# Experts 2 to 7: gathered rows transposed by VectorE after a trip through DRAM; second MLP: first two tiles transposed on TensorE

## The chip, the cores and the metric

The kernel runs on one core of one Trainium2 chip. The metric is the device time of one execution in microseconds (us). A profile of one execution stands beside the times; "span" is the time from the first to the last recorded instruction in it. Engines are called TensorE (PE; PEld is its weight load), VectorE (DVE), ScalarE (ACT), GpSimd (POOL) and SyncE (SP, which here only issues DMAs).

## What is computed

Three layers follow each other, all in float32. A linear attention (softmax of q over the head dimension, of k over the sequence) gives x, 2304 rows of 512. A mixture of eight experts with two chosen per row takes x, and a second MLP with a softmax gate and a normalisation takes its result:

```python
# attention: B, H, S, D = 4, 8, 576, 64
kv = np.einsum('bhsd,bhse->bhde', k_s, v)
x = np.einsum('bhsd,bhde->bhse', q_s, kv)          # -> 2304 x 512

# experts: D, F, E = 512, 1024, 8; two experts chosen per row
for e in range(E):
    for k in range(2):
        mask = top2[:, k] == e
        h = np.maximum(x[mask] @ w1[e], 0.0)
        out[mask] += top2_w[mask, k, None] * (h @ w2[e])

# second MLP: 512 -> 1024 -> 512
h = x @ w_in
solu = h * softmax(h)
ln = (solu - mean(solu)) / np.sqrt(var(solu) + 1e-06) * g_ln
out = ln @ w_out
```

## The kernel before

**Splitting.** Every large product is done as three products of float32r parts: an operand is cast to float32r by ScalarE (the high part, names ending in h) and the rest is formed by VectorE (the low part, names ending in l). A product takes high x high, high x low and low x high. TensorE wants both operands with the contracted index on the partitions, so activations must be transposed between layers.

**Expert stage.** Each expert has room for 640 rows, five tiles of 128. `gather_x` fetches a tile's rows from the DRAM tensor xd by an indirect DMA on GpSimd's queue. `xt_tile` transposes it: `transpose_split` does four 128x128 transposes on TensorE into one of two PSUM banks (tile name t), ScalarE casts them to xh, VectorE subtracts to xl (lines 732, 734, 735). The loop `for e in range(1, E)` first runs the first product of expert e in eight parts (`mm1`, line 756: 24 matmuls of 320 columns each), whose results ScalarE and VectorE turn into hh and hl (lines 760, 761), and then the second product in five tiles (`mm2`, line 792: 24 matmuls of 512 columns). Ahead of each of these five tiles stands `xt_tile(e + 1, a)`, the transposition of a row tile for the next expert. Weights come in 512 KB pieces on SyncE's queue (`load_w1`, `load_w2`, lines 146, 152) into four shared raw buffers, and are split by `split_w1` and `split_w2` (lines 161, 162, 167, 168). A background generator, `decode_all`, takes a step at most places of the loop: it loads a piece of the second MLP's weights (tile f, line 193), decodes it on VectorE (lines 201 to 216) and stores it to DRAM (line 217).

**Second MLP.** It runs over 18 tiles of 128 rows in a software pipeline, `for i in range(NC + 3)`. `h_in(i)` is the first product (line 840, 48 matmuls of two halves), `solu(i)` the softmax gate (maximum at line 849, exponential 852, product 855, mean taken off 858), `rstd(i - 1)` the statistics (lines 868 to 878), `x2_trans(i + 1)` the transposition of a later input tile on TensorE, `o_out(i - 3)` the output product (line 923). The gated activations of tile t (name ed, at the end dT) must be transposed before `o_out(t)`. For tiles 0 to 15 that goes through DRAM: `d_write` stores them (line 885), `d_read` reads them back in four DMAs, so that each group of 32 partitions holds its share of the columns (line 890), and `d_back` transposes 32x32 blocks on VectorE (line 896), casts (899) and subtracts (900). For the last two tiles `d_trans` does eight transposes on TensorE instead (line 910).

Every engine works through its own instructions in the order in which the program wrote them, and a DMA queue likewise: an issue that waits holds back what stands behind it. At the end of the expert stage stands a branch for rows that do not fit into 640 places (`overflow`).

Of the kernel before, what the change touches and what calls it, by code (L numbers as in the profile page):

```python
# [8 lines left out]
F32 = mybir.dt.float32  # L9
# [11 lines left out]
NT, DM, FF, E = 2304, 512, 1024, 8  # L21
R = 4
NC = NT // 128
NL = S - 128 * R
KD, KF = DM // 128, FF // 128
NA = 5
# [21 lines left out]
def col_rows(t):  # L48

    j, c = divmod(t, 9)  # L50
    if c == 8:
        return [(64 * u, 64, (2 * j + u) * S + 128 * R, 1) for u in range(2)]
    return [(0, 128, (2 * j + c // R) * S + c % R, R)]

ORDER = """
F:100011101100000000100000000000101111 lk:0 lq:0 lkl:0 lk:1 kr:0 kmt:0 qm:0 lvl:0 km:0:0 klt:0 kl:0 km:0:1 kb:0
# [26 lines left out]
def attn_moe_kernel(ctx: ExitStack, tc: tile.TileContext, q, k, v, w_gate, w_noise, noise,  # L83
                    w1, w2, w_in, w_out, g_ln, out, order=None, stop=False):
    nc = tc.nc
    V, A, P, T, SP = nc.vector, nc.scalar, nc.gpsimd, nc.tensor, nc.sync
# [5 lines left out]
    dram = ctx.enter_context(tc.tile_pool(name="dram", bufs=1, space=DRAM))  # L92
    sb = ctx.enter_context(tc.tile_pool(name="sb", bufs=1))

    def slot(tag, shape, dt, name):
        return sb.tile(shape, dt, tag=tag, name=name)

    def ring(*tags):
        state = [-1]

        def take(shape, dt, name):
            state[0] = (state[0] + 1) % len(tags)
            return slot(tags[state[0]], shape, dt, name)
        return take

    new_raw = ring("R2", "R3", "R0", "R1")
    new_row = ring("S0", "S2", "S4", "S1", "S3")
    new_out = ring("S9", "S8", "S10")
    new_s2 = ring("S5", "S6", "S7", "S11")
    psA = ctx.enter_context(tc.tile_pool(name="psA", bufs=2, space=PSUM))  # L110
    psB = ctx.enter_context(tc.tile_pool(name="psB", bufs=2, space=PSUM))
# [4 lines left out]
    tab = dram.tile([OVT * 128, 2], I32, name="tab")  # L116
    win32 = dram.tile([DM, FF], F32, name="win32")
    wout32 = dram.tile([FF, DM], F32, name="wout32")
    dd = [dram.tile([128, FF], F32, name=f"dd{t}") for t in range(NC - 2)]

    def bank_t():
        return psT.tile([128, 512], F32, tag="t", name="t")
# [4 lines left out]
    def bank_b():  # L127
        return psB.tile([128, 512], F32, tag="b", name="b")
# [13 lines left out]

    def load_w1(e, j):
        t = new_raw([128, KD, 256], F32, "raw")
        src = win32 if e == E else w1[e]
        SP.dma_start(out=t, in_=src[:, 256 * j:256 * j + 256].rearrange("(k p) f -> p k f", p=128))
        raw[1, e, j] = t

    def load_w2(e, j):
# [313 lines left out]
    eTs, xs = {}, {}  # L463
# [68 lines left out]
    Gt = {}  # L532
# [186 lines left out]
    xg = {}  # L719

    def gather_x(e, a):
        t = new_row([128, DM], F32, "xg")
        c = E * a + e
        first = e == 0 and a < TA
        P.indirect_dma_start(out=t, out_offset=None, in_=xd[0:NRA, :] if first else xd, in_offset=bass.IndirectOffsetOnAxis(  # L725
            ap=idxA[:, a:a + 1] if first else idx[:, c:c + 1], axis=0))
        xg[e, a] = t

    def transpose_split(t, hi, lo):
        ps = bank_t()  # L730
        for kk in range(KD):
            T.transpose(ps[:, 128 * kk:128 * kk + 128], t[:, 128 * kk:128 * kk + 128], ident)  # L732
        pv = ps.rearrange("p (k t) -> p k t", k=KD)
        A.copy(hi, pv)  # L734
        V.tensor_sub(lo, pv, hi)  # L735

    XT = {}

    def xt_tile(e, a):
        if a == 0:  # L740
            XT[e] = (slot("XH", [128, KD, CAP], F32R, "xh"), slot("XL", [128, KD, CAP], F32R, "xl"))
        hi, lo = XT[e]
        transpose_split(xg.pop((e, a)), hi[:, :, 128 * a:128 * a + 128], lo[:, :, 128 * a:128 * a + 128])

    hT = {}

# [56 lines left out]
    def col_of(t):  # L803

        return t if t < NC - 2 else 2 * NC - 3 - t
# [39 lines left out]
    def solu(t):  # L845
        pa = hb.pop(t)
        c = col[:, t]
        pf = pa.rearrange("p n f -> p (n f)")
        V.reduce_max(c[:, 0:1], pf, axis=AX, negate=True)  # L849
        ed = new_ed([128, 2, FF], F32, "ed")  # L850
        e, d = ed[:, 0], ed[:, 1]
        A.activation(out=e, in_=pf, func=AF.Exp, bias=c[:, 0:1], accum_out=c[:, 1:2])  # L852
        V.tensor_scalar(c[:, 2:3], c[:, 1:2], 1e-9, None, op0=OP.add)
        V.reciprocal(c[:, 2:3], c[:, 2:3])  # L854
        V.scalar_tensor_tensor(d, pf, c[:, 2:3], e, op0=OP.mult, op1=OP.mult, accum_out=c[:, 3:4])  # L855
        V.tensor_scalar(c[:, 4:5], c[:, 3:4], -1.0 / FF, None, op0=OP.mult)
        if t < NC - 2:
            V.tensor_scalar(d, d, c[:, 4:5], None, op0=OP.add)
        else:
            V.tensor_scalar(e.rearrange("p (k g c) -> p g k c", g=4, k=KF), d.rearrange(  # L860
                "p (g k c) -> p g k c", g=4, k=KF), c[:, 4:5], None, op0=OP.add)
            e, d = d, e
        rsd[t] = e, d, c[:, 7:8]
# [20 lines left out]
    def d_write(t):  # L884
        SP.dma_start(out=dd[t], in_=rsd[t][1])
# [17 lines left out]
    def d_trans(t):  # L903
        d = rsd[t][1]
        dt = new_dT([128, 2, KF, 128], F32R, "dT")
        for i in range(2):
            ps = bank_t()
            for k in range(4):
                c = 512 * i + 128 * k
                T.transpose(ps[:, 128 * k:128 * k + 128], d[:, c:c + 128], ident)  # L910
            pv = ps.rearrange("p (k t) -> p k t", k=4)
            hi, lo = (dt[:, j, 4 * i:4 * i + 4, :] for j in range(2))
            A.copy(hi, pv)
            V.tensor_sub(lo, pv, hi)
        dT[t] = (dt[:, 0], dt[:, 1])

    def o_out(t):
        hi, lo = dT.pop(t)
        pb = bank_b()
        for kk in range(KF):  # L920
            wh, wl = (w[:, kk % 2, :] for w in WO[kk // 2])
            for s, (x, w) in enumerate(((hi, wh), (hi, wl), (lo, wh))):
                T.matmul(pb, lhsT=x[:, kk, :], rhs=w, start=(kk == 0 and s == 0),  # L923
                         stop=(kk == KF - 1 and s == 2))
        y = rsd.pop(t)[2]
        o = new_out([128, DM], F32, "o")
        if t < NC - 1:
            A.activation(out=o, in_=pb, func=AF.Copy, scale=y)
        else:
            A.activation(out=o[:, 0:256], in_=pb[:, 0:256], func=AF.Copy, scale=y)  # L930
            V.tensor_scalar(o[:, 256:512], pb[:, 256:512], y, None, op0=OP.mult)  # L931
        for p0, n, row, st in col_rows(col_of(t)):
            dst = out[row:row + n, :] if st == 1 else out[row - row % S:row - row % S + st * n, :].rearrange(
                "(p r) d -> p r d", r=st)[:, row % S, :]
            SP.dma_start(out=dst, in_=o[p0:p0 + n, :])
# [191 lines left out]
    for e in range(1, E):  # L1127
        for m in range(KF):
            mm1(e, m)
            if m < 4:  # L1130
                split_w2(e, m)
                load_w1(e + 1, m)
            if e + 1 < E and m < NA:
                gather_x(e + 1, m)
            if m >= 3:
                next(bg, None)
            if e == 2 and m == 5:
                pair_gates()
                count_overflow()
        if stop:  # L1140
            return
        for a in range(NA):
            if e + 1 < E:
                xt_tile(e + 1, a)
            mm2(e, a)
            if e < E - 1:
                next(bg, None)
                if a < 4:
                    split_w1(e + 1, a)
                    load_w2(e + 1, a)  # L1150
                continue
            gather_y(a)
            if a < 2:
                for j in (2 * a, 2 * a + 1):
                    split_w1(E, j)
                    load_w2(E, j)
            elif a == 2:
                next(bg, None)
                combine(0)
                split_w2(E, 0)  # L1160
            elif a == 3:
                x2_trans(0)
                combine(1)
                split_w2(E, 1)
# [7 lines left out]
    for i in range(NC + 3):  # L1172
        if i < NC:
            h_in(i)
        if 0 <= i - 1 < NC - 2:
            d_read(i - 1)
        if 0 <= i - 2 < NC - 2:
            d_back(i - 2)
        if 2 <= i < NC - 1:
            x2_trans(i + 1)  # L1180
        if i < NC:
            solu(i)
        if i < NC - 2:
            d_write(i)
        if i == 0:
            x2_trans(2)
        if i < NC - 3:
            combine(i + 3)
        if i == 1:
            split_w2(E, 3)  # L1190
        if 1 <= i <= NC:
            rstd(i - 1)
        if i >= 3:
            o_out(i - 3)
        if i in (NC - 1, NC):
            d_trans(i - 1)
        if i + 5 < NC:
            gather_y(i + 5)
# [31 lines left out]
```

## Time and profile before

| | us |
|---|---|
| three runs, median (lowest to highest) | 815.04 (814.2 to 815.2) |
| the profiled execution | 813.08 |
| span of the profiled execution | 811.3 |
| TensorE busy | 756.5 |
| VectorE busy | 504.0 |
| ScalarE busy | 293.9 |
| GpSimd busy | 147.1 |

The DMA engines move 150 GB/s on average. Times of instructions below are counted from the start of the span. Matmuls overlap: one that is listed with 0.40 us may be followed by the next after 0.23, so that the length of a stretch on TensorE is read from starts, not from durations.

### The profile page before, as it was taken

How to read it: one execution, taken by the hardware profiler on the slowest of the kernel's cores; microseconds unless marked ns; L12 is line 12 of the kernel's file. 1: busy time of each engine (PE TensorE's matmuls, PEld its weight loads, DVE VectorE, ACT ScalarE, POOL GpSimd, SP SyncE). 2: the span in 40 equal slices, each digit the busy share in tenths (PEclk: the TensorE clock that was granted, in tenths of full speed). 3: DMA queues.
4: the chain of work that ended last, by engine and by line, in shares of the span. 5: the costliest groups of instructions: out<-in, count | busy, mean ns of one | idle time of the engine just before them, and what ended most of it. 6: DMA issues, size and time to landing. Idle time of an engine off the chain costs nothing. (4 is left out here: it accounts for less than half of the span.)

```text
span 811.3 us, 12471 instructions
## 1 busy us (share of the span) xinstructions
PE 756.5 (93%) x4918; PEld 682.5 (84%) x4918; DVE 504.0 (62%) x884; ACT 293.9 (36%) x484; POOL 147.1 (18%) x130
## 2 busy tenths in 40 slices
PE   2877859999999999999999999999988999999997
PEld 1776858989889889899899899898777999899986
DVE  5899783335656656657646656555466777767661
ACT  1566531333223223223232332231444444444441
POOL 3584563020110110200100200000341211200000
PEclk9998899999999999999999999999997999999999
DMA  9973444264454443554544452532754645543311
GB/s 266 269 249 118 143 158 143 79 195 156 134 178 130 144 157 129 170 168 128 177 137 141 170 168 79 162 119 90 219 167 156 179 151 164 156 144 130 107 50 39
DMA packets 82974, 122.07 MB, mean 150 GB/s; under 512 B 15072, under 2 KB 53984, under 8 KB 82912
## 3 DMA queue, kind: packets, MB, share of 16 engines
q1 hardware_dynamic: 76832, 101.32, 39.3%
q0 software_dynamic: 6080, 19.93, 8.7%
q8 instruction: 39, 0.64, 0.3%
q14 instruction: 23, 0.19, 0.1%
HBM read 88.72 MB, written 32.51 MB: 149 GB/s over the span
## 5 line engine op out<-in xcount | busy, mean ns | idle before, releaser
L756 PE MATMUL a<-xh,w1h 128*128 128x320 f32 x448 | 138.6, 309 | 1.2 <-DVE hl L761 1.2
L756 PE MATMUL a<-xl,w1h 128*128 128x320 f32 x448 | 138.4, 309 | 0.0
L756 PE MATMUL a<-xh,w1l 128*128 128x320 f32 x448 | 138.4, 309 | 0.0
L792 PE MATMUL b<-w2h,hh 128*128 128x512 f32 x320 | 128.8, 402 | 0.0
L792 PE MATMUL b<-w2h,hl 128*128 128x512 f32 x320 | 126.7, 396 | 0.0
L792 PE MATMUL b<-w2l,hh 128*128 128x512 f32 x320 | 126.3, 395 | 0.0
L760 ACT ACTIVATE hh<-a 128x640 fp32r<-128x640 f32 x56 | 39.5, 706 | 159.9 <-PE a L756 159.9
L725 POOL DMA_INDIRECT xg<-xd,idx x38 | 40.7, 1070 | 304.1 <-PE t L732 294.7
L761 DVE SCALAR_TENSOR_TENSOR hl<-a,hh 128x640 fp32r<-128x640 f32 x56 | 46.1, 823 | 64.8 <-ACT hh L760 64.8
L756 PEld LDWEIGHTS a<-xh,w1h 128*128 128x128 f32 x448 | 84.1, 188 | 1.8 <-DVE hl L761 1.4
L756 PEld LDWEIGHTS a<-xl,w1h 128*128 128x128 f32 x448 | 84.1, 188 | 0.4
L756 PEld LDWEIGHTS a<-xh,w1l 128*128 128x128 f32 x448 | 84.2, 188 | 0.0
L815 POOL DMA_INDIRECT yg<-yd,posi x36 | 37.7, 1048 | 212.4 <-DVE w1l L162 100.1
L792 PEld LDWEIGHTS b<-w2h,hl 128*128 128x128 f32 x320 | 60.0, 187 | 13.9
L792 PEld LDWEIGHTS b<-w2l,hh 128*128 128x128 f32 x320 | 60.2, 188 | 13.0
L792 PEld LDWEIGHTS b<-w2h,hh 128*128 128x128 f32 x320 | 60.2, 188 | 12.6
L840 PE MATMUL a<-w1h,x2h 128*128 128x256 f32 x288 | 58.3, 284 | 7.8 <-ACT x2h L734 7.3
L162 DVE TENSOR_TENSOR w1l<-raw,w1h 128x1024 fp32r<-128x1024 f32 x32 | 38.9, 1222 | 33.5 <-ACT w1h L161 33.5
L840 PE MATMUL a<-w1h,x2l 128*128 128x256 f32 x288 | 57.8, 282 | 0.2 <-DVE x2l L735 0.2
L840 PE MATMUL a<-w1l,x2h 128*128 128x256 f32 x288 | 57.7, 282 | 0.0
L794 DVE COPY yo<-b 128x512 f32<-128x512 f32 x24 | 16.6, 691 | 64.2 <-PE b L792 64.2
L923 PE MATMUL b<-w2x,dT 128*128 128x512 f32 x216 | 54.4, 400 | 0.0
(209 smaller groups left out, 1395.1 us busy)
## 6 DMA issues: line engine op xcount, KB each, us to landing
raw<-in_moe_w_dram SPq DMA_DIRECT2D x64, 512.0 KB
yd<-yo SPq DMA_DIRECT2D x40, 256.0 KB
dd<-ed SPq DMA_DIRECT2D x16, 512.0 KB
dq<-dd SPq DMA_DIRECT2D x64, 128.0 KB
k<-in_k_dram SPq DMA_DIRECT2D x4, 1024.0 KB
q<-in_q_dram SPq DMA_DIRECT2D x4, 1024.0 KB
v<-in_v_dram SPq DMA_DIRECT2D x4, 1024.0 KB
xd<-xr SPq DMA_DIRECT2D x8, 512.0 KB
```

The source lines that it names most:

```text
L162: (pick_engine(20 + j, P, V) if e == 0 else V).tensor_sub(W1l[j], t, W1h[j])
L725: P.indirect_dma_start(out=t, out_offset=None, in_=xd[0:NRA, :] if first else xd, in_offset=bass.IndirectOffsetOnAxis(ap=idxA[:, a:a + 1] ...
L756: T.matmul(pa[:, n, 0:HC], lhsT=a, rhs=b, start=(kk == 0 and s == 0), stop=(kk == KD - 1 and s == 2))
L760: A.activation(out=h2, in_=pa[:, :, 0:HC], func=AF.Relu)
L761: V.scalar_tensor_tensor(l2, pa[:, :, 0:HC], 0.0, h2, op0=OP.max, op1=OP.subtract)
L792: T.matmul(pb, lhsT=x, rhs=y, start=(kk == 0 and s == 0), stop=(kk == KF - 1 and s == 2))
L794: (A.copy if a % 2 else V.tensor_copy)(t, pb)
L815: P.indirect_dma_start(out=r, out_offset=None, in_=yd[0:n, :], in_offset=bass.IndirectOffsetOnAxis(ap=posi[:, c, j:j + 1], axis=0))
L840: T.matmul(pa[:, n, 256 * c:256 * c + 256], lhsT=x[:, kk, :], rhs=w[2 * n + c][:, kk, :], start=(kk == 0 and s == 0 and c == 0), stop=(kk ...
L923: T.matmul(pb, lhsT=x[:, kk, :], rhs=w, start=(kk == 0 and s == 0), stop=(kk == KF - 1 and s == 2))
```

## The change

Two constants come in: EQ = 2 and NP = 2.

For experts EQ to 7, `gather_x` puts the rows into one of three new buffers, which have the names of attention tiles that are no longer in use. `write_x` stores them to DRAM, `read_x` reads them back with four DMAs of 64 KB, one for each group of 32 partitions, and `xt_tile` has VectorE transpose 32x32 blocks into one of two buffers; ScalarE and VectorE then split from there. Since the contracted index lies differently on the partitions in that form, the first weights of these experts are loaded in four DMAs too. In the loop of expert e the write of tile a is issued at part a + 1 of the first product, the read at part a + 3. For tiles 0 to NP - 1 of the second MLP the activations are transposed by `d_trans`, and `o_out` of these two tiles is called one step earlier; in step 4 there is none.

```diff
-        src = win32 if e == E else w1[e]
-        SP.dma_start(out=t, in_=src[:, 256 * j:256 * j + 256].rearrange("(k p) f -> p k f", p=128))
+        src = (win32 if e == E else w1[e])[:, 256 * j:256 * j + 256]
+        if e < EQ or e == E:
+            SP.dma_start(out=t, in_=src.rearrange("(k p) f -> p k f", p=128))
+        else:
+            for g in range(4):
+                SP.dma_start(out=t[32 * g:32 * g + 32], in_=src[128 * g:128 * g + 128].rearrange("(k c) f -> c k f", c=32))
...
-        t = new_row([128, DM], F32, "xg")
+        t = (new_row if e < EQ else new_hop)([128, DM], F32, "xg")
...
+    def write_x(e, a):
+        SP.dma_start(out=xs_d[e, a], in_=xg[e, a])
+
+    def read_x(e, a):
+
+        t = xg[e, a] = new_row([128, DM], F32, "xg")
+        for g in range(4):
+            SP.dma_start(out=t[32 * g:32 * g + 32].rearrange("i (b f) -> i b f", b=4),
+                         in_=xs_d[e, a].rearrange("(b i) f -> i b f", i=32)[:, :, 128 * g:128 * g + 128])
...
-        transpose_split(xg.pop((e, a)), hi[:, :, 128 * a:128 * a + 128], lo[:, :, 128 * a:128 * a + 128])
+        hi, lo = (x[:, :, 128 * a:128 * a + 128] for x in XT[e])
+        t = xg.pop((e, a))
+        if e < EQ:
+            transpose_split(t, hi, lo)
+            return
+        x = slot(("S12", "Gt")[a % 2], [128, KD, 4, 32], F32, "xt")
+        V.transpose(x.rearrange("p k b i -> p b k i"), t.rearrange("p (b k c) -> p b k c", b=4, k=KD))
+        x = x.rearrange("p k b i -> p k (b i)")
+        A.copy(hi, x)
+        V.tensor_sub(lo, x, hi)
...
+            if EQ <= e + 1 < E:
+                if 1 <= m < NA + 1:
+                    write_x(e + 1, m - 1)
+                if 3 <= m:
+                    read_x(e + 1, m - 3)
...
-        if 0 <= i - 1 < NC - 2:
+        if i == 1:
+            d_trans(0)
+        if NP <= i - 1 < NC - 2:
             d_read(i - 1)
-        if 0 <= i - 2 < NC - 2:
+        if NP <= i - 2 < NC - 2:
             d_back(i - 2)
...
-        if i >= 3:
+        if 2 <= i < 2 + NP:
+            o_out(i - 2)
+        if i >= 3 + NP:
             o_out(i - 3)
-        if i in (NC - 1, NC):
+        if i in (NP, NC - 1, NC):
             d_trans(i - 1)
```

How the instructions stand now is shown at three places. Line numbers of the changed kernel are higher by up to 37.

SyncE's queue, loop of expert 1, before: gl are the normalisation's factors, raw a piece of weights, f the first pieces to be decoded, win the decoded ones.

```order
L1092 DMA gl<-in_moe_g_ln_dram 32x8x1 x4
L146 DMA raw<-in_moe_w_dram 128x4x256 x4
L193 DMA f_1932<-in_moe_w_in_dram 128x1024
L193 DMA f_1934<-in_moe_w_in_dram 128x1024
L217 DMA win_78<-dec_1965 128x512
L193 DMA f_2060<-in_moe_w_in_dram 128x1024
```

The same place after; xs are the row tiles of expert 2 in DRAM.

```order
L156 DMA raw<-in_moe_w_dram 32x4x256 x8
L740 DMA xs_0_80<-xg 128x512
L156 DMA raw<-in_moe_w_dram 32x4x256 x4
L740 DMA xs_1_81<-xg 128x512
L156 DMA raw<-in_moe_w_dram 32x4x256 x4
L740 DMA xs_2_82<-xg 128x512
L746 DMA xg<-xs_0_80 32x4x128 x4
L203 DMA f_1980<-in_moe_w_in_dram 128x1024
L203 DMA f_1982<-in_moe_w_in_dram 128x1024
L740 DMA xs_3_83<-xg 128x512
L746 DMA xg<-xs_1_81 32x4x128 x4
```

Between the second and the third piece of weights stands a write, between the fourth and the first f a write and four reads.

VectorE, the same loop, between the last part of the first product and the second tile of the second, before: dec is the decoder's work, yo the copy of the output tile, w1l the low part of the next expert's weights.

```order
L216 SCALAR_TENSOR_TENSOR dec_1965<-dec_1967,dec_1965 128x512
L735 TENSOR_TENSOR xl<-t,xh 128x4x128
L794 COPY yo<-b 128x512
L201 TENSOR_SCALAR dec_2100<-f_1934 128x512
L202 SCALAR_TENSOR_TENSOR dec_2099<-f_1934,dec_2100 128x512
L203 SCALAR_TENSOR_TENSOR dec_2099<-f_1934,dec_2099 128x512
L162 TENSOR_TENSOR w1l_100<-raw,w1h_96 128x1024
L735 TENSOR_TENSOR xl<-t,xh 128x4x128
```

After:

```order
L226 SCALAR_TENSOR_TENSOR dec_2019<-dec_2021,dec_2019 128x512
L768 STREAM_TRANSPOSE xt<-xg 128x4x4x32
L771 TENSOR_TENSOR xl<-xt,xh 128x4x128
L822 COPY yo<-b 128x512
L211 TENSOR_SCALAR dec_2167<-f_1982 128x512
L212 SCALAR_TENSOR_TENSOR dec_2166<-f_1982,dec_2167 128x512
L213 SCALAR_TENSOR_TENSOR dec_2166<-f_1982,dec_2166 128x512
L172 TENSOR_TENSOR w1l_128<-raw,w1h_124 128x1024
L768 STREAM_TRANSPOSE xt<-xg 128x4x4x32
L771 TENSOR_TENSOR xl<-xt,xh 128x4x128
```

A block transpose now stands ahead of each subtraction that makes xl; nothing else changed places.

TensorE, second MLP, between the first products of tiles 2 and 3, before: the last two matmuls of tile 2, the transposes of x for tile 3 and the first matmuls of tile 3.

```order
L840 MATMUL a<-w1h_98,x2l 128x256
L840 MATMUL a<-w1h_99,x2l 128x256
L732 MATMUL t<-ident,yg 128x128 x4
L840 MATMUL a<-w1h_96,x2h 128x256
L840 MATMUL a<-w1h_97,x2h 128x256
```

After: from the transposes of x for tile 3 to those of tile 1's activations.

```order
L752 MATMUL t<-ident,yg 128x128 x4
L951 MATMUL b<-w2x,dT 128x512 x12
L951 MATMUL b<-w2h,dT 128x512
L951 MATMUL b<-w2l,dT 128x512
L951 MATMUL b<-w2h,dT 128x512 x2
L951 MATMUL b<-w2l,dT 128x512
L951 MATMUL b<-w2h,dT 128x512 x2
L951 MATMUL b<-w2l,dT 128x512
L951 MATMUL b<-w2h,dT 128x512 x2
L951 MATMUL b<-w2l,dT 128x512
L951 MATMUL b<-w2h,dT 128x512
L938 MATMUL t<-ident,ed 128x128 x8
```

The output product of tile 0 (line 951) and eight transposes of tile 1 (line 938) now stand between the two first products. Eight more transposes, of tile 0, stand ahead of the first product of tile 2.

## Rows read from the trace of the kernel before

**Rows 1.** Page, part 1: busy time, share, instructions.

```profile
PE 756.5 (93%) x4918; PEld 682.5 (84%) x4918; DVE 504.0 (62%) x884; ACT 293.9 (36%) x484; POOL 147.1 (18%) x130
```

**Rows 2.** Windows: stretch, length, busy PE, PEld, DVE, ACT, POOL, clock, DMA share.

```profile
290.00:345.00 55.00, 55.00 (x317) 49.99 (x317) 32.68 (x46) 16.55 (x23) 5.44 (x5) 1.00 0.45 141
122.00:126.00 4.00, 3.79 (x23) 3.79 (x23) 2.94 (x13) 0.38 (x1) 0.00 (x0) 0.57 0.00 0
612.00:617.00 5.00, 4.85 (x21) 4.55 (x22) 3.66 (x6) 2.65 (x4) 0.00 (x0) 0.50 0.33 105
```

**Rows 3.** Timeline (start, length, engine, line, operation, idle before), start of second MLP.

```profile
600.74 2.21 SPq L890 DMA_DIRECT2D dq<-dd  x4
608.96 1.25 DVE L896 STREAM_TRANSPOSE dq<-dq 128x1024 f32<-128x1024 f32 x1 [1.46 <-DMA dq<-dd]
611.87 0.79 PE L840 MATMUL a<-w1h,x2h 128*128 128x256 f32 x2 [7.31 <-ACT x2h L734]
613.10 1.22 DVE L849 TENSOR_REDUCE col<-a 128x1 f32<-128x1024 f32 x1
620.05 0.16 DVE L878 TENSOR_TENSOR col<-col 128x1 f32<-128x1 f32 x1
620.30 0.60 PE L732 MATMUL t<-ident,yg 128*128 128x128 f32 x4
624.33 1.21 DVE L849 TENSOR_REDUCE col<-a 128x1 f32<-128x1024 f32 x1
```

**Rows 4.** Timeline of TensorE: transposes ahead of two tiles, loop of expert 3.

```profile
329.63 0.60 PE L732 MATMUL t<-ident,xg 128*128 128x128 f32 x4
335.65 0.60 PE L732 MATMUL t<-ident,xg 128*128 128x128 f32 x4
```

**Rows 5.** Timeline of TensorE: second product of the last expert, first four tiles.

```profile
556.64 0.40 PE L792 MATMUL b<-w2h,hh 128*128 128x512 f32 x1
...
578.98 0.60 PE L732 MATMUL t<-ident,yg 128*128 128x128 f32 x4
```

**Rows 6.** Timeline, three engines: first and fifth tile, loop of expert 6.

```profile
501.52 0.68 DVE L735 TENSOR_TENSOR xl<-t,xh 128x512 fp32r<-128x512 f32 x1
...
522.45 0.60 PE L732 MATMUL t<-ident,xg 128*128 128x128 f32 x4
524.08 0.59 ACT L734 CAST xh<-t 128x512 fp32r<-128x512 f32 x1
524.22 1.23 DVE L162 TENSOR_TENSOR w1l<-raw,w1h 128x1024 fp32r<-128x1024 f32 x1 [1.97 <-ACT w1h L161]
525.36 0.68 DVE L735 TENSOR_TENSOR xl<-t,xh 128x512 fp32r<-128x512 f32 x1
528.47 0.31 PE L756 MATMUL a<-xh,w1h 128*128 128x320 f32 x1
```

**Rows 7.** SyncE's issues (timeline), and the landing times of the row gathers.

```profile
476.94 10.92 SPq L146 DMA_DIRECT2D raw<-in_moe_w_dram  x4
611.39 1.73 SPq L890 DMA_DIRECT2D dq<-dd  x4
DMA to landing us min/median/max: 3.3/4.1/6.5
```

**Rows 8.** Timeline, first decode loads and what waits; last, an earlier TensorE wait.

```profile
194.51 2.44 SPq L193 DMA_DIRECT2D f<-in_moe_w_in_dram  x2
200.18 0.43 DVE L201 TENSOR_SCALAR dec<-f 128x512 uint32<-128x512 uint32 x1 [3.93 <-DMA f<-in_moe_w_in_dram]
202.85 0.42 PE L756 MATMUL a<-xh,w1h 128*128 128x320 f32 x1 [1.16 <-DVE hl L761]
122.21 0.18 PE L636 MATMUL t<-M,tri 128*128 128x40 f16 x1 [3.79 <-DVE M L632]
```

**Rows 9.** Chain that ended last (start, length, engine, tile, line).

```profile
626.49 5.55 PE a L840 x48
788.41 0.87 PE t L910 x8
```

More of the change, by code (lines that the diff above doesn't have):

```diff
@@ L53, in col_rows @@
     return [(0, 128, (2 * j + c // R) * S + c % R, R)]
+NP = 2
+EQ = 2
 ORDER = """
@@ L108, in attn_moe_kernel @@
     new_out = ring("S9", "S8", "S10")
+    new_hop = ring("RH0", "RH1", "RH2")
     new_s2 = ring("S5", "S6", "S7", "S11")
@@ L118, in attn_moe_kernel @@
     wout32 = dram.tile([FF, DM], F32, name="wout32")
-    dd = [dram.tile([128, FF], F32, name=f"dd{t}") for t in range(NC - 2)]
+    xs_d = {(e, a): dram.tile([128, DM], F32, name=f"xs{e}_{a}") for e in range(EQ, E) for a in range(NA)}
+    dd = {t: dram.tile([128, FF], F32, name=f"dd{t}") for t in range(NP, NC - 2)}
     def bank_t():
@@ L741, in xt_tile @@
             XT[e] = (slot("XH", [128, KD, CAP], F32R, "xh"), slot("XL", [128, KD, CAP], F32R, "xl"))
-        hi, lo = XT[e]
-        transpose_split(xg.pop((e, a)), hi[:, :, 128 * a:128 * a + 128], lo[:, :, 128 * a:128 * a + 128])
+        hi, lo = (x[:, :, 128 * a:128 * a + 128] for x in XT[e])
[8 more added lines that the diff above has]
+        V.tensor_sub(lo, x, hi)
     hT = {}
@@ L856, in solu @@
         V.tensor_scalar(c[:, 4:5], c[:, 3:4], -1.0 / FF, None, op0=OP.mult)
-        if t < NC - 2:
+        if NP <= t < NC - 2:
             V.tensor_scalar(d, d, c[:, 4:5], None, op0=OP.add)
@@ L1182, in attn_moe_kernel @@
             solu(i)
-        if i < NC - 2:
+        if NP <= i < NC - 2:
             d_write(i)
```

## The prediction

> **What bounds the kernel now.** I read the page's engine totals first: TensorE is busy 93% of the span, VectorE 62%, ScalarE 36% [rows 1]. Then busy time by stretch: in the middle of the expert stage TensorE is busy 55.00 of 55.00 us at full clock, VectorE 32.7, and the DMA engines at a share of 0.45 [rows 2]. There the time is what TensorE has in its queue; whatever leaves the queue comes off the end, as long as nothing else becomes late. The third view is the order of time where the second MLP begins: TensorE waits 7.31 us until 611.87 [rows 3], and then runs at the lower of its two levels (granted clock 0.50, 1.2 GHz) until about 617 [rows 2]. These are the two places that the change touches.
>
> **Part 1: the transposes of experts 2 to 7 leave TensorE.** A row tile costs four transposes and, for another expert, one tile of the second product. From one tile's transposes to the next tile's is 335.65 - 329.63 = 6.02 us [rows 4]. The last expert runs four such tiles without transposes from 556.64 to 578.98, 5.585 us each [rows 5]. So a tile's transposes cost TensorE 0.435 us. Six experts of five tiles: 30 x 0.435 = **13.05 us less**.
>
> What comes in for it is free only if it is on time. *VectorE.* A 128x1024 block transpose takes 1.25 us [rows 3], so I take 0.62 for half the width; cast and subtraction I leave at today's 0.59 and 0.68 [rows 6], though they will read SBUF instead of PSUM. The tightest place is the fifth tile, whose subtraction must end before the next expert's first matmul. It stands behind the last weight subtraction on VectorE, and that behind ScalarE's weight cast. Before: TensorE is through with the fourth tile at 522.45, the weight subtraction leaves VectorE at about 525.4, the low part ends at 526.0, TensorE arrives at 528.47 [rows 6]. After: 525.4 + 0.62 + 0.64 + 0.7 = 527.36 (each hand-over 0.05 us or less), while TensorE arrives 0.435 us sooner, at 528.03. The margin shrinks from 2.4 to 0.7 us but holds: I cost it at nothing. Each microsecond beyond the margin would cost six.
>
> *SyncE's queue.* Per expert it gets 12 more weight loads (four parts for one), 5 writes and 20 reads. An issue of such a part takes 0.43 us (four in 1.73) [rows 7]; with a write at the same price, 37 x 0.43 = 16 us in a loop of 58 us. The four weight loads of a loop are issued over 10.92 us [rows 7], paced by VectorE, which frees a buffer every 3.5 us; four issues and a write fit between two. After the fourth, at 487.5 us, stand its three other parts, a write and the four reads of tile 0: 8 x 0.43 = 3.4 us, so they are out by 491. VectorE comes to tile 0 at 501.5 [rows 6]. The slowest landing that I see for such a set is 6.0 us after the last issue (600.74 + 2.21 = 602.95, used at 608.96) [rows 3]. So 4 us are left. GpSimd's gathers now wait for the writes that free their three buffers, and the writes of tiles 3 and 4 wait for those gathers; behind a waiting write in SyncE's queue stand reads that are wanted 10 us later or more, and a decode load that has a whole tile's decoding in reserve. Cost nothing.
>
> *One place in the queue costs something.* In the loop of expert 1, the first loads of the weights to be decoded stand behind the fourth weight load. VectorE waits 3.93 us for the first of them, the low part of a hidden tile stands behind that, and TensorE waits 1.16 us for it [rows 8]. The change puts three weight parts, a write and four reads ahead of these loads: 8 x 0.43 = 3.4 us later. Of the load's 5.67 us to landing (194.51 to 200.18) [rows 8] some is other traffic; the least that I see for a gather is 3.3 us [rows 7], so up to 2.4 us may come back. Bounds of the term: 1.0 and 3.4, and on top what a long wait does to the clock: after a wait of 3.79 us [rows 8] the granted clock was 0.57 over the next 4 us [rows 2], worth 1.7 us. I take **2.5 us more**, bounds 1.0 and 5.1.
>
> The Trainium skill speaks against this part: VectorE: DVE Perf Modes, section Rules for kernel authors, wants a 128x128 transpose on TensorE where PSUM will do as the destination. The rows say that in this stage TensorE has no time left and VectorE 40%; by the page's rule VectorE would become the bound, which is a rival below.
>
> **Part 2: the first two tiles of the second MLP.** Before, TensorE ends the first product of tile 2 at about 604 and then waits for the split x of tile 3. On ScalarE and VectorE that split stands behind tile 0's activations, which come back from DRAM and are transposed at 608.96 only. The next product starts at 611.87 and lasts to 620.30, 8.43 us [rows 3]; the one after it takes 5.55 [rows 9]. So 7.31 us of waiting and 2.88 of slow clock, **10.2 us**, hang on that trip. After, tiles 0 and 1 need no DRAM; the output product of tile 0 (5.6 us) stands where TensorE waited, and x of tile 3 is split before it ends. The clock then has no long wait ahead of it to fall after.
>
> Added on TensorE: two times eight transposes, 0.87 us for eight [rows 9]: **1.7 us**. New waits, (a): TensorE's transposes share two banks. The casts of tile 1's activations stand behind the statistics of that tile; from a maximum to the end of those statistics VectorE needs 7.1 us (613.10 to 620.21) [rows 3]. With the maximum of tile 2 moved up to about 610, the second cast and subtraction are through at about 610 + 7.1 + 1.3 = 618.4; TensorE wants a bank for x of tile 4 after, from 604.0 on, eight transposes, the output product of tile 0, eight transposes and a first product, 604.0 + 0.9 + 5.6 + 0.9 + 5.6 = 617.0: 1.4 us. (b): Between the products of tiles 4 and 5 there is no output product any more. TensorE needs 6.0 us there, VectorE 11.2 a tile (maximum at 613.10, next at 624.33) [rows 3]; of the 5.2 us between them most is the lead that the products have, and I take 1.4. Together **2.8 us**, bounds 0 and twice that. From tile 6 on the order is that of before. Part 2: -10.2 + 1.7 + 2.8 = **-5.7 us**, bounds -8.5 and -2.9.
>
> **Sum.** -13.05 + 2.5 - 5.7 = -16.2 us. The profiled execution took 813.08 us, 811.3 of them span: 796.9 for it. The median of the three runs, 815.04, is 1.96 above that execution; against the median I predict **798.8 us**.
>
> **The rivals.**
> *Expert 1's queue costs more.* The late decode load drops the clock too, and the 0.7 us margin at the fifth tile is missed by 0.5 us in six loops. Then part 1 brings 13.05 - 5.1 - 3.0 = 5.0 and the whole 10.7: 804.3 us. For it: that wait exists already. Against: only the first decode load is urgent.
> *Part 2 brings nothing.* VectorE's 11.2 us a tile are close to TensorE's (5.55 + 5.6 + 0.44 = 11.6), so what TensorE gains at 604 could be taken back over the next tiles; 13.05 - 2.5 = 10.5 us are left: 804.5 us. Against: the maximum starts 4 us after its product's end (620.30, 624.33) [rows 3], but TensorE needs its result two products later only.
> *VectorE becomes the bound of the expert stage.* Around the fifth tile it has an idle piece of 1.97 us [rows 6]; transposition and wait for ScalarE take 1.3 of such a piece. If the block transpose took 2.0 us instead of 0.62, the fifth tile would be late by 0.7, 4 us in six loops: 803 us. The skill's rule above leads here. For it: a price at half width that no row shows. Against: the row at full width is 1.25 us.
> *Slower than before.* The reads of the fifth tile land late in every loop, and TensorE waits at each expert's first matmul. This decides from 0.7 + 16.2/6 = 3.4 us behind the time when VectorE wants the tile. At 5 us behind, with a fall of the clock each time (1.7 us), it is 6 x (4.3 + 1.7) = 36 us: 835 us. For it: 20 small reads a loop behind writes that wait for gathers. Against: they are issued some 25 us ahead, the slowest landing is 6.0.
> *The transposes were free*, because something else sets TensorE's pace: then part 1 gives -2.5 and part 2 is eaten by its waits, 815 us. The four tiles without transposes [rows 5] speak against it.
>
> **How the numbers follow.** Forecast 0.70; expert 1's queue 0.10; part 2 nothing 0.08; VectorE the bound 0.05; slower 0.04; nothing 0.03. The bounds of the terms give -13.05 + 1.0 - 8.5 = -20.6 (794.5 us) and -13.05 + 5.1 - 2.9 = -10.9 (804.2 us); the three milder rivals lie between 803 and 804.5. The range is 794.5 to 805. About 0.2%, 1.6 us, is what a measurement can tell from no change. Faster 0.93, same 0.03, slower 0.04.
>
> **What would show it.** After about 205 us no transposes of gathered rows on TensorE, and tiles of the second product of 5.585 us in every expert; a TensorE wait of 2 to 5 us before the last first product of expert 1; around the start of the second MLP no wait over 2 us and no granted clock near 0.5, with the output product of tile 0 ahead of the first product of tile 3. I would be wrong if TensorE waited at the first matmul of experts 2 to 7, if VectorE waited for the reads, or if the waits after tile 3 added up to 10 us.

## The result and the profile after

The changed kernel takes 823.13 us (median of four runs, 820.11 to 826.23) beside 814.62 us of the kernel before: a ratio on record of 1.0115, interval 1.0079 to 1.0151 (the two medians by themselves give 1.0104). It is **slower by 1.15%**; forecast were 798.8 us. The profiled execution has a span of 819.9 us, 8.6 more than before.

The page's totals, as in [rows 1]:

```profile
PE 755.7 (92%) x4814; PEld 681.5 (83%) x4814; DVE 522.2 (64%) x914; ACT 296.3 (36%) x486; POOL 142.9 (17%) x130
```

TensorE has 104 instructions less and is busy as long as before (756.5): the matmuls of the experts' first product alone are listed with 424.2 us in place of 415.4. The trace of its stages says why. The second MLP, from its first product to the last matmul, takes 219.89 us before and 213.41 after, 6.5 less. The six loops of experts 1 to 6 take 351.6 us before and 366.6 after, 15.0 more. Lengths of these loops, from the first matmul of the first product to the next such one (the last three rows are experiments, below):

| loop of expert | 1 | 2 | 3 | 4 | 5 | 6 | sum |
|---|---|---|---|---|---|---|---|
| before | 59.69 | 58.83 | 58.30 | 58.25 | 58.27 | 58.24 | 351.6 |
| changed | 64.28 | 58.35 | 61.90 | 62.52 | 63.46 | 56.10 | 366.6 |
| e1 | 64.38 | 56.64 | 56.10 | 56.09 | 56.09 | 56.10 | 345.4 |
| e5 | 56.09 | 56.65 | 56.10 | 56.09 | 56.09 | 56.09 | 337.1 |
| e9 | 56.10 | 58.57 | 61.79 | 59.30 | 62.96 | 56.08 | 354.8 |

The loop of expert 6 is what was forecast, 58.24 - 2.17 = 56.07. The others lose time, and the view of waits of the changed kernel names it. A row gives the engine, the instruction that waits and what it waits for, then us in total, times, longest. First TensorE:

```profile
PE a L784 <- DVE hl L789: 14.3, 3, 5.4
PE b L820 <- DVE hl L789: 5.5, 2, 4.0
```

19.8 us of waits for hl, the low part of a hidden tile, where the kernel before has the 1.16 us of [rows 8]. And VectorE, same view:

```profile
DVE dec L211 <- DMA win<-dec: 20.1, 3, 8.6
DVE dec L211 <- DMA wout<-dec: 13.0, 3, 7.6
DVE dec L211 <- DMA f<-in_moe_w_in_dram: 8.2, 1, 8.2
```

L211 is the first instruction of decoding a piece of weights. Only 8.2 us of its waits are for a load; 33.1 us are for the **store** of the piece before. The order of time around one of them, loop of expert 5 of the changed kernel, on SyncE's queue, then VectorE, then TensorE (start, us, instruction, idle before it and what ended it):

```profile
441.52 1.74 SPq L156 DMA_DIRECT2D raw<-in_moe_w_dram  x4
443.36 0.38 SPq L740 DMA_DIRECT2D xs<-xg  x1
443.78 2.08 SPq L746 DMA_DIRECT2D xg<-xs  x4
445.96 0.38 SPq L227 DMA_DIRECT2D wout<-dec  x1
...
441.87 0.69 DVE L226 SCALAR_TENSOR_TENSOR dec<-dec,dec 128x512 f32<-128x512 uint32 x1
442.85 0.82 DVE L789 SCALAR_TENSOR_TENSOR hl<-a,hh 128x640 fp32r<-128x640 f32 x1 [0.29 <-ACT hh L788]
451.32 0.43 DVE L211 TENSOR_SCALAR dec<-f 128x512 uint32<-128x512 uint32 x1 [7.64 <-DMA wout<-dec]
...
453.11 0.82 DVE L789 SCALAR_TENSOR_TENSOR hl<-a,hh 128x640 fp32r<-128x640 f32 x1
...
453.99 0.64 PE L784 MATMUL a<-xh,w1h 128*128 128x320 f32 x1 [4.93 <-DVE hl L789]
```

VectorE is through with the piece at 442.56 (441.87 + 0.69). The store is issued at 445.96, behind four weight parts (one load before the change), a write and four reads, and has landed at 451.32. Until then L211 stands, behind it the next hl, and behind that TensorE. The same place before (VectorE, SyncE's queue, VectorE):

```profile
429.57 0.69 DVE L216 SCALAR_TENSOR_TENSOR dec<-dec,dec 128x512 f32<-128x512 uint32 x1
...
430.29 0.34 SPq L217 DMA_DIRECT2D wout<-dec  x1
...
433.76 0.43 DVE L201 TENSOR_SCALAR dec<-f 128x512 uint32<-128x512 uint32 x1 [2.38 <-DMA wout<-dec]
```

There the store is issued 0.03 us after the piece is done and lands 3.47 us later. VectorE waits too, but 2.38 us, and TensorE does not notice.

Why the next piece waits for the store is in the decoder, which the change does not touch:

```python
new_s2 = ring("S5", "S6", "S7", "S11")
a, b, c = (new_s2([128, 512], U32, f"dec{j}") for j in range(3))
V.tensor_scalar(b, hw, 3, 0x3FFFFFF8, ...)     # first instruction, L211
...
SP.dma_start(out=dst[rs, c0:c0 + 512], in_=af) # the store of a, L227
```

A piece takes three of four buffers in turn: a, b, c are S5, S6, S7, and for the next piece S11, S5, S6. So the next piece's first instruction writes into the buffer whose store is under way.

Each of the four waits of 4 us and more is followed by a lower clock (0.52, 0.57, 0.54 and 0.51 in windows of 4 to 7.5 us); for the one above (stretch, us, busy us and instructions by engine, granted clock, DMA share, GB/s):

```profile
447.00:452.00 5.00, 2.06 (x15) 1.79 (x13) 0.65 (x2) 0.70 (x1) 0.94 (x1) 1.00 1.04 335
452.00:459.00 7.00, 5.01 (x19) 5.01 (x20) 5.30 (x9) 0.00 (x0) 2.12 (x2) 0.51 0.83 230
```

### The profile page after: what moved, and what is told of

It reads as the page before. It is cut to its first block, busy times and chain, and to the rows that moved or that the text cites. A ratio compares the mean times of both kernels' runs of the same rounds, so it can differ in the third digit from the quotient of the medians.

```text
span 819.9 us, 12578 instructions
## 1 busy us (share of the span) xinstructions
PE 755.7 (92%) x4814; PEld 681.5 (83%) x4814; DVE 522.2 (64%) x914; ACT 296.3 (36%) x486; POOL 142.9 (17%) x130
## 5 line engine op out<-in xcount | busy, mean ns | idle before, releaser
L784 PE MATMUL a<-xh,w1h 128*128 128x320 f32 x448 | 141.8, 317 | 14.3 <-DVE hl L789 14.3
L784 PE MATMUL a<-xl,w1h 128*128 128x320 f32 x448 | 141.3, 315 | 0.0
L784 PE MATMUL a<-xh,w1l 128*128 128x320 f32 x448 | 141.1, 315 | 0.0
L784 PEld LDWEIGHTS a<-xh,w1h 128*128 128x128 f32 x448 | 86.8, 194 | 15.4 <-DVE hl L789 15.1
L735 POOL DMA_INDIRECT xg<-xd,idx x38 | 38.1, 1004 | 348.9 <-DMA xs<-xg 337.3
L784 PEld LDWEIGHTS a<-xl,w1h 128*128 128x128 f32 x448 | 86.7, 194 | 0.4
L784 PEld LDWEIGHTS a<-xh,w1l 128*128 128x128 f32 x448 | 86.7, 194 | 0.0
L820 PEld LDWEIGHTS b<-w2l,hh 128*128 128x128 f32 x320 | 60.7, 190 | 14.3
L843 POOL DMA_INDIRECT yg<-yd,posi x36 | 35.8, 994 | 181.5 <-DVE w1l L172 72.7
L770 ACT CAST xh<-xt 128x512 fp32r<-128x512 f32 x30 | 18.6, 620 | 107.1 <-DVE xt L768 107.1
L951 PE MATMUL b<-w2h,dT 128*128 128x512 f32 x144 | 48.1, 395 | 0.0
```

Source lines behind the costliest of these rows:

```text
L770: A.copy(hi, x)
L784: T.matmul(pa[:, n, 0:HC], lhsT=a, rhs=b, start=(kk == 0 and s == 0), stop=(kk == KD - 1 and s == 2))
L820: T.matmul(pb, lhsT=x, rhs=y, start=(kk == 0 and s == 0), stop=(kk == KF - 1 and s == 2))
L843: P.indirect_dma_start(out=r, out_offset=None, in_=yd[0:n, :], in_offset=bass.IndirectOffsetOnAxis(ap=posi[:, c, j:j + 1], axis=0))
```

## The experiments

The theory is this store; the rivals are VectorE's work itself, the traffic on the DMA engines, and a first part whose gain was never there. All ratios are to the kernel before.

**e1: another buffer for the result.** The only wait taken away is that for the store.

```diff
-        a, b, c = (new_s2([128, 512], U32, f"dec{j}") for j in range(3))
+        a, b, c = (slot(g, [128, 512], U32, f"dec{j}") for j, g in enumerate((("S5", "S11")[i % 2], "S6", "S7")))
```

> The result of a decoding goes to one of two buffers by turns, and the two scratch buffers are always the same, so that the next decoding no longer writes first into the buffer whose store is still under way. Nothing else changes. Theory (store): in the changed kernel TensorE lost 1.7 + 5.8 + 6.4 + 7.4 = 21.3 us in the loops of experts 2 to 5 behind VectorE, and VectorE stood there at the first instruction of a decoding until the store of the one before had landed (4.8, 6.7, 8.6, 7.6 us). The waits on a store go, and with them about 21 us: 823 - 21 = 802 us. The wait of 8.2 us for the first load in the loop of expert 1 stays. Rival (VectorE has too much work): the waits move to another instruction, and the time stays within 3 us of the changed kernel, 820 to 826. Rival (DMA traffic): VectorE waits for a load of the pieces to be decoded or for the rows read back instead; 812 or more.

Measured: 800.27 us, 0.9832 (0.9795 to 0.9868). Loops 3 to 6 last 56.1 us, loop 2 56.6, and of the waits one of each kind is left (view of waits, e1):

```profile
PE a L784 <- DVE hl L789: 6.6, 1, 6.6
...
DVE dec L211 <- DMA f<-in_moe_w_in_dram: 9.4, 1, 9.4
```

All DMAs and all of VectorE's work are still there. The theory holds with its number.

**e2: the decoding called ahead of the rows' DMAs.**

```diff
+            if m >= 3:
+                next(bg, None)
             if EQ <= e + 1 < E:
                 if 1 <= m < NA + 1:
                     write_x(e + 1, m - 1)
                 if 3 <= m:
                     read_x(e + 1, m - 3)
-            if m >= 3:
-                next(bg, None)
```

> In a step of the expert loop the decoding, with its store and its next load, is called ahead of the write and the reads of the rows and not behind them: on SyncE's queue the store stands one write and four reads further ahead, the first loads in the loop of expert 1 as well. VectorE's order is unchanged. If the place in the queue is what makes the store late, its issue comes some 3 us sooner (one write and four reads, 0.4 + 2.5 us), and so the long waits of TensorE shrink by about 3 us each: 3 x 3 us in experts 3 to 5, 4 us in expert 1, and part of the slow clock after each: 823 - 13 = 810 us. If what makes it late is the landing (3.5 to 7 us, other traffic), the issue alone brings less: 818 or more. If VectorE's work is the bound, nothing: 823.

Measured: 804.59 us, 0.9886 (0.9839 to 0.9934): 18.5 us off the changed kernel, more than the 13 expected. The store of the loop of expert 5, SyncE's queue of e2:

```profile
427.90 1.75 SPq L156 DMA_DIRECT2D raw<-in_moe_w_dram  x4
429.75 0.38 SPq L227 DMA_DIRECT2D wout<-dec  x1
...
431.31 3.44 SPq L746 DMA_DIRECT2D xg<-xs  x4
```

Three stores, in the loops of experts 3, 4 and 5, show both parts of the delay. From the end of the piece to the issue they take together 0.1 us before, 11.6 in the changed kernel (4.4, 3.8, 3.4) and 2.6 in e2; from the issue to VectorE's next instruction 9.8 before, 16.1 changed (3.5, 7.2, 5.4) and 14.3 in e2. So the place in the queue is the larger part, and the longer landing is most of what e2 leaves. TensorE waits 7.8 us for hl in e2 in place of 19.8, 2.8 at most. The six loops take 18.0 us less than in the changed kernel; 12.0 of these are the waits; the other 6.0 are time after them, where the granted clock is low for shorter. Of that the expectation had counted only a part.

**e3: no transposes on VectorE.**

```diff
-        V.transpose(x.rearrange("p k b i -> p b k i"), t.rearrange("p (b k c) -> p b k c", b=4, k=KD))
-        x = x.rearrange("p k b i -> p k (b i)")
+        x = t.rearrange("p (k i) -> p k i", k=KD)
```

> Leaves out VectorE's block transposes of experts 2 to 7 (30 x 0.70 us = 21 us of VectorE's work); the cast and the subtraction take the rows as they were read back. All DMAs stay. Theory (store): VectorE stands and waits where the time is lost, so its work is not what is missing: 821 to 823 us, no more than 2 us less. Rival (VectorE has too much work): the greater part of the 28 us lost in the expert loops comes back, 795 to 808 us.

This kernel leaves the block transposes out, so it computes something else; it is here for its time. Measured: 821.5 us, 1.0095 (1.0065 to 1.0124). 21 us of work off VectorE bring 1.6 by the medians, which the two intervals do not tell from nothing: VectorE was not the bound, it stood and waited.

**e4 and e8: the two parts apart.** e4 sets NP to 0 and takes the steps of the second MLP as they were; e8 sets EQ to 8.

> Only the first part of the change; the second MLP is as before. By the traces the expert loops of the changed kernel take 15 us longer and the second MLP 6.5 us less, so 814.6 + 15 = 830 us, if the two parts do not touch each other. If the second MLP gains because the expert stage left it in another state, the time would be near the changed kernel's 823.

> Only the second part of the change; the expert stage is as before. By the traces the second MLP takes 219.89 us before and 213.41 after: 813.2 - 6.5 = 806.7 us. If its gain hung on the first part, the time would be that of the kernel before.

Measured: e4 827.84 us, 1.0168 (1.0131 to 1.0205), where 830 were expected; e8 806.91 us, 0.9916 (0.9895 to 0.9938), where 806.7 were. Within the intervals the parts add up and do not touch each other: 14.7 - 6.4 = 8.3, and the whole change costs 8.5.

**e5: e1, and the first two loads of the decoder ahead of expert 1's loop.**

```diff
     bg = decode_all()
+    next(bg)
...
-            if m >= 3:
+            if m >= 3 and (e, m) != (1, 3):
                 next(bg, None)
```

> The alternating result buffer, and the first two loads of the pieces to be decoded issued ahead of the loop of expert 1 (they stood in its fourth step). With the alternating buffer alone the loops of experts 2 to 6 last 56.1 us, that of expert 1 64.4. If the 8.3 us between them is the late first load and the clock after it, they go: 800.3 - 8.3 = 792 us. If they are a load that SyncE's queue holds back, of whatever kind, VectorE or TensorE waits for another DMA in that loop and the time stays over 797.

Measured: **793.02 us**, 0.9739 (0.9718 to 0.9760), the fastest of all. At the place shown above, SyncE's queue and VectorE in e5:

```profile
420.72 1.75 SPq L156 DMA_DIRECT2D raw<-in_moe_w_dram  x4
422.57 0.50 SPq L740 DMA_DIRECT2D xs<-xg  x1
423.12 1.96 SPq L746 DMA_DIRECT2D xg<-xs  x4
425.19 0.37 SPq L227 DMA_DIRECT2D wout<-dec  x1
...
421.07 0.69 DVE L226 SCALAR_TENSOR_TENSOR dec<-dec,dec 128x512 f32<-128x512 uint32 x1
422.06 0.82 DVE L789 SCALAR_TENSOR_TENSOR hl<-a,hh 128x640 fp32r<-128x640 f32 x1 [0.30 <-ACT hh L788]
422.80 0.42 DVE L211 TENSOR_SCALAR dec<-f 128x512 uint32<-128x512 uint32 x1
```

The store is as late as in the changed kernel (421.76 to 425.19, 3.4 us), but L211 runs ahead of its issue. No one waits for it.

**e6: e1's edit in the kernel before.**

> The kernel before with the alternating result buffer and nothing else. It waited 7.4 us on VectorE for stores, in four waits, and its loops of experts 1 to 6 held 2.0 us over the pace of their instructions, most of it (1.4) in that of expert 1, whose wait is for a load. So up to 0.6 us: 813 us, no change that can be told. Rival (the buffer is a gain by itself, whatever the change does): the loops of experts 2 to 6 become shorter than 58.2 us each, 808 or less.

Measured: 813.50 us, 1.0009 (0.9992 to 1.0026). The buffers cost the kernel before nothing; only the change made them dear.

**e7: the rows' writes and reads issued by GpSimd.** `P.dma_start` for `SP.dma_start` in write_x and read_x.

> The changed kernel with the writes and reads of the rows issued by GpSimd and not by SyncE; the decoding keeps its one ring of buffers. The traffic is the same, SyncE's queue is rid of 25 issues a loop and of the writes that wait for a gather. If the place in the queue makes the stores late: VectorE's waits on stores fall from 33 us towards the 7.4 of the kernel before, that for the first load from 8.2 to some 5, and the time is 823 - 28 + 4 = 799 us. If the landing under the added traffic does it: the waits stay at 20 us or more, 810 to 823 us. If GpSimd is too slow in issuing, VectorE waits for xg at its transposes, and TensorE at the first product of experts: slower than 823.

Measured: 797.27 us, 0.9791 (0.9764 to 0.9819). VectorE's waits at L211 for stores fall to 8.8 us (3.3, 0.2, 2.8, 2.5), its wait for the first load to 5.9. SyncE's queue of e7, at the same store:

```profile
418.26 8.78 SPq L156 DMA_DIRECT2D raw<-in_moe_w_dram  x12
427.14 0.38 SPq L227 DMA_DIRECT2D wout<-dec  x1
```

The weight loads in four parts are still ahead of it; issued 0.8 us after the end of its piece (426.33), it has landed 3.2 us later (430.30). The same three stores as in e2 take 2.5 us together from the end of the piece to the issue and 8.5 from there to VectorE's next instruction, less than the 9.8 before. One thing in this run is not what I meant it to be: GpSimd has none of SyncE's other work in its queue. It runs ahead, its reads wait only for buffers that VectorE's transposes free (153.6 us in all), and so they are issued in the second product instead of beside the stores. So e7 moves the traffic in time as well and does not separate queue and traffic; e2 does that for the queue.

The Trainium skill, DMA: Bandwidth & Descriptors, section Issuing engines are not separate DMA queues, says that issuing from several engines saves only the sequencer's time for the issue, which is usually small beside the DMA itself. Here the issues moved are 25 a loop of about 0.5 us, and moving them brought 26 us: behind them stood a store with someone waiting, and the reads no longer ran beside it. How much each of the two brought is not shown by this run.

**e9: the early loads alone, on the changed kernel**, with the diff of e5.

> The changed kernel with the first two loads of the pieces to be decoded ahead of the loop of expert 1, and with its one ring of buffers. The loop of expert 1 took 64.3 us and would take 56.1; the waits on stores in experts 2 to 5 stay: 823 - 8 = 815 us. It gives the price of expert 1's term by itself: 64.3 less the 57.5 that the loop would take at the delay of before (59.69 - 2.17), so 6.8 us, where the prediction took 2.5. If the lost time moves on to the next waits, less than 5 us come back.

Measured: 813.86 us, 1.0000 (0.9976 to 1.0024); loop 1 is at 56.10 us. Its ten runs lie between 808.7 and 817.5 us, the four of e5 between 792.3 and 793.5. That with the stores late the time depends on how each landing turns out is my reading of this; one execution of each kernel has a trace, so it is not shown run by run. One place where the two traces part is loop 4. There TensorE waits 2.95 us where the changed kernel waits 4.03, and the clock after it differs (the changed kernel, then e9; columns as above):

```profile
397.00:404.50 7.50, 5.06 (x13) 4.01 (x14) 6.62 (x12) 1.56 (x2) 0.00 (x0) 0.54 0.21 53
```

```profile
388.00:395.00 7.00, 5.73 (x25) 4.66 (x26) 6.19 (x11) 1.57 (x2) 0.00 (x0) 1.00 0.31 82
```

The granted clock is 0.54 after the one, close to the lower level of 1.2 GHz, and 1.00 after the other. The loop is 62.52 us long in the one and 59.30 in the other, 3.2 us apart, of which 1.1 are the wait. The length of the wait alone does not say which clock follows; the last section has the rows of e2 on that.

**e10: e5 without the first part** (EQ = 8).

> The fastest version with the first part of the change taken out again: alternating result buffer, first loads ahead of expert 1's loop, second part of the change. By the second part alone (806.9) less the 1.7 us that its loop of expert 1 holds over the 58.25 of the others: 805 us. The difference to the version with the first part (793.0) is then the price of the 30 tiles' transposes with no wait behind it: 12 to 13 us, where the prediction took 13.05. If it is 8 or less, the term itself was too large.

Measured: 804.88 us, 0.9885 (0.9862 to 0.9907). Its six loops sum to 350.1 us, those of e5 to 337.1: the transposes' price is 13.0 us by the traces, 11.9 by the medians.

## Why the prediction was wrong

The measured change is made of the same terms as the forecast, with one more: -13.0 for the transposes, +21.3 for the stores, +6.7 for expert 1's load, -6.5 for part 2, 8.5 us together.

**Transposes, -13.05 us: right.** 13.0 between e10 and e5.

**VectorE and the fifth tile, 0: right.** A block transpose of half width took more than the 0.62 us that I took (view of one line, changed kernel; ns least/median/most), and the margin of 0.7 us came out as 0.6: in e5 the last low part ends at 458.96 and TensorE starts the next expert at 459.55. VectorE waits for no read of a row: the list of what ended its idle time before L768 is empty.

```profile
L768 DVE STREAM_TRANSPOSE xt<-xg x30: 703/705/707, 216.3 to 541.1; 128x512 f32<-128x512 f32 x30
```

The Trainium skill, VectorE: DVE Perf Modes, section Rules for kernel authors, would leave a 128x128 transpose on TensorE where PSUM will do as the destination. e10 and e5 differ by 11.9 us the other way: here the measurement decides. It is of the whole way, the trip through DRAM and the block transposes, with nobody waiting for the DMAs. TensorE had no time left in this stage, and VectorE had.

**SyncE's queue, "cost nothing": the step that failed.** It cost 21.3 us in the loops of experts 2 to 5 (1.7, 5.8, 6.4 and 7.4 over those of e5). I counted 37 issues a loop, asked who waits for the rows and for the *loads* behind them, and found "a decode load that has a whole tile's decoding in reserve". That is true of the load. The store in the same queue I did not follow to the one who waits for it: the next decoding, which writes into its buffer. The trace of before had that wait (2.38 us in the rows above); I read VectorE's wait for the first load, [rows 8], as the only urgent one, because TensorE felt no other. Its margin can be read: 2.7 us of VectorE's wait stay hidden from TensorE (7.64 - 4.93 above; 6.71 - 4.00 in the loop of expert 3), and the kernel before used 2.4 of them. In the loops of experts 2 and 4, where TensorE stands in the second product, 3.4 and 4.6 stay hidden (4.82 - 1.45, 8.58 - 4.03). I never worked that out, and 3.4 to 4.4 us in the queue and up to 4.5 in the landing went past it.

**Expert 1's load, +2.5 us (1.0 to 5.1): right in kind, too small.** The loop lost 64.28 - 56.09 = 8.19 us, before 59.69 - 58.24 = 1.45: 6.7 us. The loads are issued 5.5 us later, not 3.4 (194.51, 200.00). Reads take 2.87 us for four where I took the 1.73 of the four reads of dq in [rows 7], and 0.6 us of gaps stand between the issues; of the landing 1 us came back (4.7 for 5.67). TensorE waits 5.39 us in place of 1.16, and what the clock then costs is 2.8 us (8.19 - 5.39), not 1.7. e9 gives the term in the same size. This was the first part of the first rival, at 6.7 us for its 5.1; its second part, the missed margin at the fifth tile, did not come. The rows, SyncE's queue, VectorE and TensorE in the changed kernel:

```profile
196.81 2.87 SPq L746 DMA_DIRECT2D xg<-xs  x4
200.00 0.88 SPq L203 DMA_DIRECT2D f<-in_moe_w_in_dram  x2
...
204.72 0.43 DVE L211 TENSOR_SCALAR dec<-f 128x512 uint32<-128x512 uint32 x1 [8.16 <-DMA f<-in_moe_w_in_dram]
...
207.39 0.64 PE L784 MATMUL a<-xh,w1h 128*128 128x320 f32 x1 [5.39 <-DVE hl L789]
```

**Part 2, -5.7 us: right.** -6.5 in the trace, -6.4 in e8. Waits of TensorE in the second MLP, changed kernel:

```profile
PE a L868 <- ACT x2h L754: 0.7, 1, 0.7
PE t L752 <- DVE dT L942: 0.6, 1, 0.6
```

The 7.3 us of [rows 3] are gone, and the granted clock is 1.00 from 602 to 650. For new waits 2.0 us are left where I took 2.8: -10.2 + 1.7 + 2.0 = -6.5. In e4 the old wait is back with 7.1 us.

**The other rivals.** Part 2 brings nothing: no (e8). VectorE as the bound: no (e3). Transposes that were free: no (e10); by its own terms, 2.5 us more and nothing from part 2, that rival's time would have been 817.5 and not 815. The slower side had one mechanism, reads that land late, and none did. The true one needed the same question put to each DMA behind the new issues. None of the three signs of being wrong came either: no wait at the first matmul of experts 2 to 7, none of VectorE for the reads, no 10 us after tile 3. They asked for the waits that I had thought of.

## What to carry to other kernels

When a queue gets new entries, go through everything that stands behind them, stores too, and for each name the instruction that waits for its landing; a store holds its buffer, so in a ring that one is the next writer. A wait that costs nothing today shows slack that is partly used up: read the waits of engines that are not the bound as margins. Before giving up a change that made something late, look whether the waiter can do without it: another order of four buffers turned this one from +1.15% to -1.7%, and with two loads moved ahead to -2.6%.

## What was not expected of the hardware

The three stores of 256 KB (loops 3 to 5) land in 2.7 to 3.6 us in the kernel before, at DMA shares of 0.66 to 0.97, and in 3.5 to 7.2 in the changed one, at 0.96 to 1.02: two of the three at hardly busier engines, and the slowest 7.22 us where the same store took 2.75. In e7, whose reads run elsewhere, they land in 2.6 to 3.2 at 0.70 to 1.06. So the share of busy time does not say how long a store lands; what in the reads beside it does is not shown.

A TensorE wait of 4.03 us was followed by a granted clock of 0.54 over 7.5 us, one of 2.95 us at the same place by 1.00, and 2.1 us of the loop's length went with that clock. But it was not the length of the wait alone: in e2 waits of 2.83, 2.75 and 2.19 us, in this order, were followed by 0.72, 1.00 and 0.76, the shortest of them by matmuls at the lower level (columns as above):

```profile
205.00:211.00 6.00, 5.16 (x25) 5.16 (x26) 4.17 (x8) 0.00 (x0) 3.07 (x3) 0.72 0.88 268
322.00:328.00 6.00, 5.02 (x30) 4.76 (x31) 4.71 (x9) 0.70 (x1) 2.11 (x3) 1.00 0.58 171
437.00:444.00 7.00, 6.39 (x30) 6.18 (x31) 4.18 (x8) 0.70 (x1) 2.84 (x3) 0.76 0.83 237
```
